# Two layers of memory attention and gMLP on one core: the lead units' turned features move into the tails of four block tiles, the second layer's first mixing operand lies over wo alone, and w_in's last load goes in two parts

## The chip, the cores and the metric

The kernel runs on one NeuronCore of one Trainium2 chip. The metric is the device time of one execution in microseconds. Every comparison is between executions of the kernel before and of another kernel on the same chip.

## The reference

Two layers run one after the other. Each is an attention with a running memory over 4 segments of 512 rows, followed by a gMLP. S = 2048 rows, D = 640, H = 32 heads of 20, Fh = 864.

```
# attention, per head and segment s: qs, ks, vs are 512 x 20; phi(t) = t + 1 for t > 0, else exp(t)
p     = softmax(qs ks^T * 20**-0.5 + mask)
num   = phi(qs) @ M                   # M, z: the memory of the segments before
o     = g * num / (phi(qs) @ z + 1e-6) + (1 - g) * p @ vs
M, z  = M + phi(ks)^T vs, z + sum(phi(ks))
x     = x + concat(o) @ wo            # q, k, v = layernorm(x) @ wq, wk, wv
# gMLP
z     = gelu(layernorm(x) @ w_in)     # 2048 x 1728
z1,z2 = z[:, :864], layernorm(z[:, 864:])
x     = x + (z1 * (w_sp @ z2 + b_sp)) @ w_out
```

## The kernel before

**Precision and tiles.** Values that go into TensorE are split into a high and a low float16 part, and a product is three matmuls (high·high, high·low, low·high). Rows come in 16 blocks t of 128. PSUM tiles are evicted by ACT and DVE; SP issues the loads, stores and transposes, all in one queue, in order.

**Phases of a layer.** `phase1a` is the attention (class `Attention`): a schedule in ticks, written by hand, lays the steps of each unit (scores, softmax, products with the values) on the engines. T is its last tick. Its late steps also carry work for what follows: the first row blocks of the gMLP's layernorm, and the load of the second half of w_in (`background`, weight `wi[0]`; the other half is `wi[1]`). The tiles of the last steps are PHL (the softmax, high and low), pv (its product with the values), oat (the divided output), ohl (its high and low part, stored to o), xt (rows of x with wo's product added, stored) and mr (row maxima for the next unit's operand qk).

`phase1b` takes each row block through the first half of the gMLP. `load` and `attn_out` bring or finish x1, layernorm gives xn. `xn_t` calls `split_t`: ACT casts the high part (L318), DVE subtracts for the low part (L319), one DMA transpose makes th (L320). `w_in_half` multiplies (zp, L395), first with `wi[1]`, then with `wi[0]` (its tile is named w in the profile). z2 is normalized and put by `blocks` into seven tiles zb, the sums and differences of a fast product scheme; z1 is stored (L409). `g.mark[i]` keeps the last instructions of step i, behind which early work of the next phase may stand on its engines (`behind`).

`phase2f` (layer 1) and `phase2s` (layer 2) mix the row blocks with w_sp: seven products per pair of blocks instead of eight (L800 and L548), then gating, and the product with w_out (cyp). w_sp's rows are scaled by their largest value, split (L764, L768, L527, L532) and turned by DMA transposes. Layer 1 stores half of the turned operand (turned), and layer 2 loads it (wt<-turned) instead of making it again. In `phase2f` a table of numbers sets the order of the items in each window: "L1" is the low half of the first combined operand (L794), "u1l" the item that ends with u<-d (L807), "P2" and "P3" the products into banks c and b.

The last window of `phase2f` also computes what layer 2's attention starts with: its two lead units' q and k (L1444), with the features phi(k) split into phl and turned into pk (L1487), and the values (L1388). mup (L1543) is the first that reads pk.

**Where the tiles lie.** SBUF has a left and a right stack of pools. On the right, from the edge, stand the tiles of `wi[1]` (17,280 bytes a partition) and of wo (12,800), then what a phase adds. Before the change layer 2's pk tiles were in a pool of 4 KB at the right edge (`nxt.pk`, pool "epk"), held until `phase2s`, and so everything that layer 2's `phase1b` puts on the right lay 4 KB further in than in layer 1, among it xnhl (pool "be1", one buffer). In `phase2s` the operand tiles wt lie on the right too: four in pt1 (16,384 bytes from the edge) and, behind it, the first two in pt0. Each zb tile has 6,912 columns; the lead units use 6,400 of them for other things, so that the last 512 are free there.

Of the kernel before, what the change touches and what calls it, by code (L numbers as in the profile page):

```python
# [9 lines left out]
F32 = mybir.dt.float32  # L10
F32R = mybir.dt.float32r
F16 = mybir.dt.float16
# [9 lines left out]
NT = S // 128  # L22
# [313 lines left out]
def phase1b(g, o_d, x, x1_d, z1_d, put, after):  # L336
    nc, tc = g.nc, g.tc
    first = not g.wu.made
    with ExitStack() as ctx:
# [66 lines left out]
        def z1_half(t, zp):  # L406
            z1 = p2.tile([128, FH], F32, tag="z1", name="z1")
            nc.scalar.activation(z1.rearrange("p (n c) -> p n c", n=2), zp[:, :, :FHH], AF.Gelu_apprx_tanh, scale=g.zi[0])
            return nc.sync.dma_start(z1_d[t], z1).ins  # L409
# [14 lines left out]
        for i, t in enumerate(ts):  # L424
            if i + 2 < NT:
                b = load(ts[i + 3]) if i + 3 < NT else None
                ths.append(xn_t(attn_out(ts[i + 2], *a)))
                a = b
            th = ths.pop(0)
            last = z2_half(t, w_in_half(1, *th))  # L430
            g.mark[i] = last
            sent = z1_half(t, w_in_half(0, *th))
            with tc.issue_after(last[1]), tc.issue_after(sent):
                if first and i in (7, 9):
                    g.wi[i == 7].keep()
                for _ in range(1 + (i < 4)):
                    next(more, None)
# [40 lines left out]
def phase2s(g, w_sp, x1_d, z1_d, zb, out):  # L478
# [6 lines left out]
    with ExitStack() as ctx:  # L485
        pool = lambda n, b, **k: ctx.enter_context(tc.tile_pool(name=n, bufs=b, reuse_waits="tile", **k))
        pr, ps, ph = pool("dr", 3), pool("ds", 2), pool("dh", 2)
        p2, px, pv, pu = pool("d2", 2), pool("dx", 3), pool("dv", 1), pool("du", 1)
        pt1, pt0 = pool("dtr1", 1, side="right"), pool("dtr0", 1, side="right")
        pg, py = pool("dg", 1, space=PSUM), pool("dy", 1, space=PSUM)  # L490
        small = lambda nm: g.small.tile([128, 1], F32, tag=nm, name=nm)
        un = g.small.tile([128, NT], F32, tag="unt", name="unt")
        nc.vector.tensor_scalar(un, g.wpw, 1.0 / (WB * ZB), None, ALU.mult)
        un = [un[:, t:t + 1] for t in range(NT)]
        raw, sums, split, ready = {}, {}, {}, {}

        def rows(t):
# [227 lines left out]
def phase2f(g, w_sp, x1_d, z1_d, zb, out, nxt, rest):  # L725
# [14 lines left out]
    psum = lambda n: pb_.enter_context(tc.tile_pool(name=n, bufs=1, space=PSUM, reuse_waits="tile"))  # L740
    pg, py = psum("fg"), psum("fy")
    small = lambda nm: g.small.tile([128, 1], F32, tag=nm, name=nm)
    un = g.small.tile([128, NT], F32, tag="unt", name="unt")
    raw, halves, wt, f = {}, {}, {}, {}

    def scale(t):
# [231 lines left out]
            item(n, k)  # L978
    wu = g.wu.bring()
    g.wu.made = True  # L980
    for w in range(NP):
        for n, lag in order:
            k = w - lag
            if not 0 <= k < NP or (n, k) in early:
                continue
            with tc.issue_after(g.parted) if w == 0 else ExitStack():
                item(n, k)
            if w == 0 and n in ("P2", "P3", "P5", "P6"):
                next(wu)
            if w + 1 == NP and n in ("P4", "P5", "P6"):  # L990
                a = "qkv"[int(n[1]) - 4]
                nc.sync.dma_start(g.wf[a], g.wkept[a])
                if n == "P5":
                    nxt.turned()
# [18 lines left out]

    run = lambda it: [None for _ in it]
    slots.close()
    nxt.pk = side(nxt.late, "epk", 2)
    halves_ = ExitStack()
    nxt.u2 = side(halves_, "eu2", 3)
    for nm, m, o in (("q", 0, "a"), ("k", 0, "b"), ("q", 1, "c"), ("k", 1, "d")):
# [105 lines left out]
class Attention:  # L1125
# [10 lines left out]
    def __init__(self, g, x, o_d, x1_d):  # L1136
        self.g, self.nc, self.tc = g, g.nc, g.tc
        self.x, self.o_d, self.x1_d = x, o_d, x1_d
        self.st = g.st
        self.xt, self.mst = g.xt, g.mst  # L1140
        self.ctx, self.late = ExitStack(), ExitStack()
        self.ln = {}
        self.gm, self.ot = {}, {}
        self.phq = {}
        self.P, self.Pf, self.mx = {}, {}, {}
        self.pv, self.o = {}, {}
        self.wait, self.last, self.stacked = [], -1, -1
        self.held, self.readout = {}, set()
        self.now, self.later, self.rd = None, {}, set()
        self.last_of, self.marks = {}, {}  # L1150
        self.half = None
        self.normed = {}
# [42 lines left out]
    def pool(self, n, b, **k):  # L1195
        return self.ctx.enter_context(self.tc.tile_pool(name=n, bufs=b, reuse_waits="tile", **k))

    def sbuf(self):
        g, pool = self.g, self.pool
        self.u2, sk, sv = pool("au2", 2), pool("ak", 1), pool("av", 1)  # L1200
        self.pk = self.u2
        self.vs = [values_tile(g, p) for p in (sv, sk)]
        self.qk = [sk.tile([128, 2, L], F16, name=f"qk{i}") for i in range(self.NQK - 1)] + [g.qk5]
        self.p3, self.pl2, self.bg, self.e2, self.pl1, self.u4 = pool("a3", 3), pool("al2", 2), pool("abg", 2), pool("ae2", 2), pool("al1", 1), pool("au4", 4)
        self.e1 = self.e2
# [250 lines left out]
    def out(self, nm, s, m, ps):  # L1456
# [25 lines left out]
        def keys():  # L1482
            hl = self.u2.tile([128, 2, L], F16, tag="hl", name="phl")
            nc.scalar.mul(hl[:, 0], ps, g.sig)
            nc.vector.scalar_tensor_tensor(hl[:, 1], ps, g.sig, hl[:, 0], ALU.mult, ALU.subtract)  # L1485
            pk = self.pk.tile([128, 2, 4, 128], F16, tag="pk", name="pk")
            nc.sync.dma_start(pk.rearrange("p i t c -> p (i t) c"), hl.rearrange("p i c -> p (i c)"), transpose=True)  # L1487
            if self.now is None:
                self.wait.append((s, m, pk))
            else:  # L1490
                self.post(3 if self.now > 0 else 5, lambda: self.update(s, m, pk), True)
# [39 lines left out]
    def update(self, s, m, pk):  # L1531
# [2 lines left out]
        for i in range(m, min(m + 2, NU)):  # L1534
            assert s < 2 or (s - 1, i) in self.readout, (s, m, i)
        self.held[(s + 1) % 2, m] = s + 1
        pkh, pkl = pk[:, 0], pk[:, 1]
        n = len(TH[m])
        hs = slice(TH[m][0], TH[m][0] + n)
        v = self.vs[s % 2]  # L1540
# [179 lines left out]
    def run(self, nseg=NSEG):  # L1720
# [81 lines left out]
        def background():  # L1802

            g, nc = self.g, self.nc
            wi = g.wi[0]
            wi.place(g.w0)
            if first:
                yield -8
                nc.sync.dma_start(g.bsp, self.b_sp.rearrange("(t p) -> p t", p=128))
                for i, a in enumerate("qkv"):  # L1810
                    yield 20 + 4 * i
                    nc.sync.dma_start(g.wkept[a], g.wf[a])
                yield 100
                yield from other_scales(g, self.ws, (wi,), 5, 101, 2.5, "ws")
                nc.vector.tensor_scalar(g.sc[:, 8:10], g.pw[:, 4:6], 2.0 ** -24, None, ALU.mult)
            yield T - 10.5
            pace = 0.5 if first else 0.9
            for i, _ in enumerate(wi.load(self.u2, FHH, ("hl", "tmp"), False, 1)):
                yield T - 10.3 + pace * i

        def weights():

# [95 lines left out]
def interleaved_layers(ctx, tc, x, wq, wk, wv, wo, beta, w_in, w_sp, b_sp, w_out, out):  # L1918
# [4 lines left out]
    g.bsp = cp.tile([128, NT], F32, tag="bsp", name="bsp")  # L1923
    g.wpw = cp.tile([128, NT], F32, tag="wpw", name="wpw")
    g.wiv = cp.tile([128, NT], F32, tag="wiv", name="wiv")
    attn_consts(g, cp, beta)
    attn_weights(g, ctx, cp, wv, wq, wk, wo, w_in, w_out)

# [15 lines left out]
    for i in range(2):  # L1944
        z1_d = [dram(f"z1_{i}_{t}", (128, FH)) for t in range(NT)]
        rest = ExitStack()
        with ExitStack() as top:
# [1 line left out]
            zp = rest.enter_context(tc.tile_pool(name="zr", bufs=1, reuse_waits="tile"))  # L1949
            zb = {**g.zb, **{j: zp.tile([128, 2, NT // 2, FHH], F16, name=f"zb{j}") for j in ZREST}}  # L1950
            phase1b(g, o_d[i], xs[i], x1_d[i], z1_d, blocks(g, zb), att[i].after)
        if i:
            att[1].late.close()
        if i:
            phase2s(g, w_sp, x1_d[i], z1_d, zb, xs[i + 1])
            rest.close()
# [28 lines left out]
```

## Time and profile before

| | |
|---|---|
| runs | 2213.96, 2214.73, 2215.64 us; median 2214.73 |
| the profiled execution | 2213.89 us, span 2212.2 us, granted TensorE clock 0.982 |
| TensorE busy | 2075.9 us, 94% of the span, 19725 matmuls |
| VectorE, ScalarE, GpSimd busy | 74%, 55%, 49% |
| DMA | 358.38 MB, mean 162 GB/s |

A row of a list of instructions has the start, the duration, the engine, the line, the operation, what it writes and reads, the count of those run together, and in brackets the idle time of the engine just before, with what ended it. Times count from the span's start. Layer 1's attention runs to about 596 us, its `phase1b` to about 790, its `phase2f` to about 1170; layer 2's attention to about 1654, its `phase1b` to about 1865, and `phase2s` to the end.

### The profile page before, as it was taken

The numbers are of one execution on the slowest core, as the hardware profiler recorded it, in microseconds if no ns is written. First come the engines' busy times: TensorE is split into PE (matmuls) and PEld (weight loads), VectorE is DVE, ScalarE is ACT, GpSimd is POOL, SyncE is SP. The second block draws the span as 40 slices with busy tenths as digits, with TensorE's granted clock in tenths as the row PEclk, the third lists the DMA queues.
The fourth block names the chain that finished last, engine by engine and source line by source line (L and its number), as shares of the span: only waits on it lengthen the run. The fifth ranks groups of instructions, "written<-read, shape, count | busy, mean of one in ns | idle before, by whom it ended". The sixth has DMA issues, their size and how long they took to land.

```text
span 2212.2 us, 48897 instructions
## 1 busy us (share of the span) xinstructions
PE 2075.9 (94%) x19725; PEld 1252.5 (57%) x19725; DVE 1626.2 (74%) x2952; ACT 1221.0 (55%) x1490; POOL 1084.3 (49%) x704
## 2 busy tenths in 40 slices
PE   4888899999899999999999999999987998999999
PEld 2455565666555545555665556566654554555555
DVE  8678888787778888999647887877764675465464
ACT  3499888788634433233225998888862344222221
POOL 2298988888424433433313987788861242000000
PEclk9999999999999999999999999999998999999999
DMA  5626635456767887888774353345565334988884
GB/s 165 186 65 207 154 91 143 109 133 151 197 169 186 236 212 195 234 243 212 204 210 112 89 136 86 110 112 143 136 187 133 90 103 122 261 204 204 228 208 114
DMA packets 516435, 358.38 MB, mean 162 GB/s; under 512 B 410096, under 2 KB 452656, under 8 KB 511088
## 3 DMA queue, kind: packets, MB, share of 16 engines
q1 hardware_dynamic: 516208, 355.26, 61.0%
q8 instruction: 154, 2.52, 0.5%
q14 instruction: 73, 0.60, 0.1%
HBM read 159.65 MB, written 107.43 MB: 121 GB/s over the span
## 4 chain that ended last, share of the span: by engine, by line
PE 69%; DVE 9%; ACT 9%; issue 5%; DMA 5%; POOL 3%; SPq 1%; POOLq 0%; ACTq 0%; DVEq 0%
PE zp L395 16%; PE cyp L596 4%; PE cyp L871 4%; ACT P L1624 3%; PE gb L548 3%; PE pv L1677 3%; PE yps L1420 3%; PE ga L548 3%; PE vps L1388 3%; PE qps L1444 3%; PE a L800 3%; PE b L800 3%; PE mp L1617 3%; ACT PHL L1642 2%; PE kps L1444 2%
## 5 line engine op out<-in xcount | busy, mean ns | idle before, releaser
L1643 POOL TENSOR_TENSOR PHL<-P,PHL 128x1024 f16<-128x1024 f32 x310 | 660.0, 2137 | 182.0 <-ACT PHL L1642 136.8
L1624 ACT ACTIVATE P<-es,sc 128x1024 f32<-128x1024 f32 x320 | 356.5, 1114 | 93.8 <-PE es L1588 91.8
L1634 DVE TENSOR_REDUCE mx<-mp 128x2 f32<-128x1024 f32 (+2 forms) x384 | 321.2, 862 | 84.4 <-PE mp L1588 83.4
L1642 ACT CAST PHL<-P 128x1024 f16<-128x1024 f32 x320 | 333.9, 1044 | 6.3
L395 PEld LDWEIGHTS <-th 128*128 128x128 f16 x1920 | 188.6, 98 | 180.2 <-DMA th<-xnhl 16.7
L1677 PEld LDWEIGHTS <-PHL 128*128 128x128 f16 x5120 | 166.7, 96 | 58.4 <-DVE oat L1698 18.7
L800 PEld LDWEIGHTS <-wt 128*128 128x128 f16 x1344 | 132.2, 98 | 118.7 <-DVE wt L794 4.4
L548 PEld LDWEIGHTS <-wt 128*128 128x128 f16 x1344 | 131.8, 98 | 119.3 <-DMA wt<-wn 6.0
L395 PE MATMUL zp<-wi,th 128*128 128x432 f16 x960 | 183.2, 350 | 16.6 <-DVE lnve L305 16.6
L306 POOL TENSOR_TENSOR lnrs<-lnve,mhalf 128x1 f32<-128x1 f32 x78 | 49.9, 648 | 299.7 <-DVE lnve L305 249.7
L1677 PE MATMUL pv<-vs,PHL 128*128 128x41 f16 x5120 | 172.5, 181 | 21.2 <-DVE oat L1698 17.4
L395 PE MATMUL zp<-w,th 128*128 128x432 f16 x960 | 180.4, 346 | 0.0
L1444 PEld LDWEIGHTS <-zb 128*128 128x128 f16 x1200 | 103.3, 99 | 102.7 <-issue 8.7
L785 POOL TENSOR_TENSOR f<-wt 128x1024 f32<-128x1024 f16 x32 | 79.7, 2494 | 139.5 <-DVE wt L794 111.4
L1617 PEld LDWEIGHTS <-qk 64*128 64x128 f16 (+1 forms) x1728 | 65.5, 93 | 127.1 <-issue 94.0
L1617 PE MATMUL mp<-qk 60*128 60x512 f16 (+3 forms) x864 | 108.2, 304 | 17.5 <-DVE mx L1634 11.9
L1420 PE MATMUL yps<-wo,o 128*128 128x320 f16 x720 | 122.0, 307 | 0.0
L1617 PE MATMUL es<-qk 64*128 64x256 f16 (+3 forms) x864 | 106.4, 298 | 9.1 <-ACT P L1624 6.5
L871 PE MATMUL cyp<-w,ut 128*128 128x320 f16 (+1 forms) x630 | 88.1, 299 | 0.0
L1388 PE MATMUL vps<-zb,w 128*128 128x320 f16 x480 | 82.8, 304 | 4.5 <-DVE phl L1485 4.5
L764 ACT ACTIVATE wn<-wr,wiv 128x1024 f16<-128x1024 f32 x32 | 36.6, 1145 | 90.4 <-DVE wiv L752 40.3
L1631 DVE TENSOR_REDUCE mx<-mp 128x4 f32<-128x1024 f32 x64 | 77.8, 1215 | 11.2 <-PE mp L1588 11.1
(313 smaller groups left out, 4220.0 us busy)
## 6 DMA issues: line engine op xcount, KB each, us to landing
wr<-in_B_w_sp_dram SPq DMA_DIRECT2D x32, 1024.0 KB
qk<-st SPq DMA_DIRECT2D x216, 120.0 KB
z<-z SPq DMA_DIRECT2D x32, 432.0 KB
cz<-z SPq DMA_DIRECT2D x32, 432.0 KB
turned<-wt SPq DMA_DIRECT2D x24, 512.0 KB
wt<-turned SPq DMA_DIRECT2D x24, 512.0 KB
st<-qhl SPq DMA_DIRECT2D x40, 256.0 KB
st<-khl SPq DMA_DIRECT2D x40, 256.0 KB
```

The lines of the kernel that those rows point to most:

```text
L395: nc.tensor.matmul(zp[:, n, :FHH], a[:, k, :], b[:, k, c:c + FHH], start=(k == 0 and j == 0), stop=(k == KD - 1 and j == 2))
L548: nc.tensor.matmul(o[:, :FHH], wt[:, x, m, :], zb[b][:, y, m, :], start=start and i == j == 0, stop=i == NP - 1 and j == 2, skip_group_che ...
L800: nc.tensor.matmul(o[:, :FHH], w[:, x, m, :], zb[b][:, y, m, :], start=start and i == j == 0, stop=i == NP - 1 and j == 2, skip_group_chec ...
L871: nc.tensor.matmul(yp[n][:, :320], a[:kn[k], k, :], b[:kn[k], k, n * 320:(n + 1) * 320], start=(k == 0 and j == 0), stop=(k == KO - 1 and ...
L1420: nc.tensor.matmul(ps, a[:, k, :], b[:, k, c], start=(i == 0), stop=(i == 14))
L1444: nc.tensor.matmul(ps, a[:, k, c], b[:, k, :], start=(i == 0), stop=(i == 14))
L1617: nc.tensor.matmul(out[:, h, o:o + w], a[r, ac], b[r, bc], start=o == 0, stop=False, skip_group_check=True)
L1624: self.last_of["ACT"] = nc.scalar.activation(self.Pf[t], es, AF.Exp, scale=g.esc).ins
L1634: self.last_of["DVE"] = nc.vector.tensor_reduce(mx[:, e, :, i], mp[:, :, o:o + w], AX.X, ALU.max).ins
L1642: nc.scalar.copy(hl[:, 0], P)
L1643: (nc.gpsimd if t < self.T - self.TAIL or t % 2 == 0 else nc.vector).tensor_tensor(hl[:, 1], P, hl[:, 0], ALU.subtract)
L1677: nc.tensor.matmul(pv[:, i, h, 0:PVC - 1], self.P[u][:, x, h, o:o + 128], v[:, j, h0 + h, :], start=first and h == x == 0 and (u, o, i, j) ...
```

## The change

1. The pool "epk" goes. Four of the zb tiles (0, 3, 4, 1) give their last 512 columns to the lead units' pk: one half (high or low) of one unit to each. A unit's features are turned by two DMA transposes of 128x4x128 instead of one of 128x8x128. Later units keep their own tile.
2. In `phase2s` a pad "dp" of 896 bytes stands ahead of pt1, so that pt1 ends where `wi[1]` ends, and pt0 lies over wo alone.
3. The load of `wi[0]` in `background` begins at T − 28 instead of T − 10.5: in layer 1 its first eight steps (a load or a split each), in layer 2 its first four, two ticks apart; the rest follows from T − 10.3.
4. `g.mark[i]` also holds z1's store and the last block difference on POOL, so that early items of `phase2f` and `phase2s` stand behind these on SP and POOL.
5. In the first window of `phase2f` the item ("L1", −1) stands right behind ("u1l", 0).
6. The scales `un` are a constant tile, filled in layer 1 and read in layer 2, which made them again before.

```diff
--- before.py
+++ after.py
@@ -428,8 +428,8 @@
                 a = b
             th = ths.pop(0)
             last = z2_half(t, w_in_half(1, *th))
-            g.mark[i] = last
             sent = z1_half(t, w_in_half(0, *th))
+            g.mark[i] = *last, sent, g.parted
             with tc.issue_after(last[1]), tc.issue_after(sent):
                 if first and i in (7, 9):
                     g.wi[i == 7].keep()
@@ -486,12 +486,11 @@
         pool = lambda n, b, **k: ctx.enter_context(tc.tile_pool(name=n, bufs=b, reuse_waits="tile", **k))
         pr, ps, ph = pool("dr", 3), pool("ds", 2), pool("dh", 2)
         p2, px, pv, pu = pool("d2", 2), pool("dx", 3), pool("dv", 1), pool("du", 1)
+        pool("dp", 1, side="right").tile([128, 224], F32, name="dp")
         pt1, pt0 = pool("dtr1", 1, side="right"), pool("dtr0", 1, side="right")
         pg, py = pool("dg", 1, space=PSUM), pool("dy", 1, space=PSUM)
         small = lambda nm: g.small.tile([128, 1], F32, tag=nm, name=nm)
-        un = g.small.tile([128, NT], F32, tag="unt", name="unt")
-        nc.vector.tensor_scalar(un, g.wpw, 1.0 / (WB * ZB), None, ALU.mult)
-        un = [un[:, t:t + 1] for t in range(NT)]
+        un = [g.un[:, t:t + 1] for t in range(NT)]
         raw, sums, split, ready = {}, {}, {}, {}
 
         def rows(t):
@@ -740,7 +739,7 @@
     psum = lambda n: pb_.enter_context(tc.tile_pool(name=n, bufs=1, space=PSUM, reuse_waits="tile"))
     pg, py = psum("fg"), psum("fy")
     small = lambda nm: g.small.tile([128, 1], F32, tag=nm, name=nm)
-    un = g.small.tile([128, NT], F32, tag="unt", name="unt")
+    un = g.un
     raw, halves, wt, f = {}, {}, {}, {}
 
     def scale(t):
@@ -978,8 +977,10 @@
             item(n, k)
     wu = g.wu.bring()
     g.wu.made = True
+    first = [x for x in order if x != ("L1", -1)]
+    first.insert(first.index(("u1l", 0)) + 1, ("L1", -1))
     for w in range(NP):
-        for n, lag in order:
+        for n, lag in order if w else first:
             k = w - lag
             if not 0 <= k < NP or (n, k) in early:
                 continue
@@ -1013,7 +1014,8 @@
 
     run = lambda it: [None for _ in it]
     slots.close()
-    nxt.pk = side(nxt.late, "epk", 2)
+    ends = [g.zb[j].rearrange("p i m c -> p (i m c)")[:, -512:].rearrange("p (t c) -> p t c", c=128) for j in ZA]
+    nxt.places = [ends[:2], ends[2:]]
     halves_ = ExitStack()
     nxt.u2 = side(halves_, "eu2", 3)
     for nm, m, o in (("q", 0, "a"), ("k", 0, "b"), ("q", 1, "c"), ("k", 1, "d")):
@@ -1138,7 +1140,7 @@
         self.x, self.o_d, self.x1_d = x, o_d, x1_d
         self.st = g.st
         self.xt, self.mst = g.xt, g.mst
-        self.ctx, self.late = ExitStack(), ExitStack()
+        self.ctx, self.places = ExitStack(), []
         self.ln = {}
         self.gm, self.ot = {}, {}
         self.phq = {}
@@ -1198,7 +1200,6 @@
     def sbuf(self):
         g, pool = self.g, self.pool
         self.u2, sk, sv = pool("au2", 2), pool("ak", 1), pool("av", 1)
-        self.pk = self.u2
         self.vs = [values_tile(g, p) for p in (sv, sk)]
         self.qk = [sk.tile([128, 2, L], F16, name=f"qk{i}") for i in range(self.NQK - 1)] + [g.qk5]
         self.p3, self.pl2, self.bg, self.e2, self.pl1, self.u4 = pool("a3", 3), pool("al2", 2), pool("abg", 2), pool("ae2", 2), pool("al1", 1), pool("au4", 4)
@@ -1483,8 +1484,14 @@
             hl = self.u2.tile([128, 2, L], F16, tag="hl", name="phl")
             nc.scalar.mul(hl[:, 0], ps, g.sig)
             nc.vector.scalar_tensor_tensor(hl[:, 1], ps, g.sig, hl[:, 0], ALU.mult, ALU.subtract)
-            pk = self.pk.tile([128, 2, 4, 128], F16, tag="pk", name="pk")
-            nc.sync.dma_start(pk.rearrange("p i t c -> p (i t) c"), hl.rearrange("p i c -> p (i c)"), transpose=True)
+            if self.places:
+                pk = self.places.pop(0)
+                for i in range(2):
+                    nc.sync.dma_start(pk[i], hl[:, i], transpose=True)
+            else:
+                pk = self.u2.tile([128, 2, 4, 128], F16, tag="pk", name="pk")
+                nc.sync.dma_start(pk.rearrange("p i t c -> p (i t) c"), hl.rearrange("p i c -> p (i c)"), transpose=True)
+                pk = pk[:, 0], pk[:, 1]
             if self.now is None:
                 self.wait.append((s, m, pk))
             else:
@@ -1534,7 +1541,7 @@
         for i in range(m, min(m + 2, NU)):
             assert s < 2 or (s - 1, i) in self.readout, (s, m, i)
         self.held[(s + 1) % 2, m] = s + 1
-        pkh, pkl = pk[:, 0], pk[:, 1]
+        pkh, pkl = pk
         n = len(TH[m])
         hs = slice(TH[m][0], TH[m][0] + n)
         v = self.vs[s % 2]
@@ -1813,10 +1820,10 @@
                 yield 100
                 yield from other_scales(g, self.ws, (wi,), 5, 101, 2.5, "ws")
                 nc.vector.tensor_scalar(g.sc[:, 8:10], g.pw[:, 4:6], 2.0 ** -24, None, ALU.mult)
-            yield T - 10.5
-            pace = 0.5 if first else 0.9
-            for i, _ in enumerate(wi.load(self.u2, FHH, ("hl", "tmp"), False, 1)):
-                yield T - 10.3 + pace * i
+            n, pace = (9, 0.85) if first else (5, 0.9)
+            yield T - 28
+            for i, _ in enumerate(wi.load(self.u2, FHH, ("hl", "tmp"), False, 1), 1):
+                yield T - 28 + 2 * i if i < n else T - 10.3 + pace * (i - n)
 
         def weights():
 
@@ -1923,6 +1930,7 @@
     g.bsp = cp.tile([128, NT], F32, tag="bsp", name="bsp")
     g.wpw = cp.tile([128, NT], F32, tag="wpw", name="wpw")
     g.wiv = cp.tile([128, NT], F32, tag="wiv", name="wiv")
+    g.un = cp.tile([128, NT], F32, tag="un", name="un")
     attn_consts(g, cp, beta)
     attn_weights(g, ctx, cp, wv, wq, wk, wo, w_in, w_out)
 
@@ -1950,8 +1958,6 @@
             zb = {**g.zb, **{j: zp.tile([128, 2, NT // 2, FHH], F16, name=f"zb{j}") for j in ZREST}}
             phase1b(g, o_d[i], xs[i], x1_d[i], z1_d, blocks(g, zb), att[i].after)
         if i:
-            att[1].late.close()
-        if i:
             phase2s(g, w_sp, x1_d[i], z1_d, zb, xs[i + 1])
             rest.close()
         else:
```

The order of the instructions follows. TensorE's rows stand as before. ACT at the end of layer 2's attention, before: the last softmax casts, the last output cast, and then the three casts of row blocks for th, the load of the gelu's table and the first gelu.

```order
L1642 CAST PHL<-P 128x1024
L1624 ACTIVATE P<-es,sc 128x1024
L1642 CAST PHL<-P 128x1024
L1708 CAST ohl<-oat 128x640
L318 CAST xnhl<-x_25822 128x640
L318 CAST xnhl<-x_25834 128x640
L318 CAST xnhl<-x_25841 128x640
L401 ACT_TABLE_LOAD
L401 ACTIVATE z_25906<-zp_25875,sc 128x864
```

The same engine after, in two pieces: behind the last mr, some eight PHL casts earlier, and at the end.

```order
L1659 ACTIVATE mr<-mtp 16x128
L318 CAST xnhl<-x_25819 128x640
L1649 CAST PHL<-P 128x1024
L1631 ACTIVATE P<-es,sc 128x1024
```

```order
L1631 ACTIVATE P<-es,sc 128x1024
L318 CAST xnhl<-x_25831 128x640
L1649 CAST PHL<-P 128x1024
L318 CAST xnhl<-x_25838 128x640
L1715 CAST ohl<-oat 128x640
L401 ACT_TABLE_LOAD
```

The first cast has moved ahead of eight of the softmax casts, the second ahead of the last of them, the third ahead of the last output cast.

SP at the end of layer 2's `phase1b`, before: z1's stores, then the loads of turned operands, then the transposes of the new ones (wn is their split form).

```order
L409 DMA z_1_9<-z_27467 128x864
L409 DMA z_1_10<-z_27550 128x864
L539 DMA wt<-turned_1 128x2048
L539 DMA wt<-turned_0 128x2048
L539 DMA wt<-turned_1 128x2048
L500 DMA wr<-in_B_w_sp_dram 128x2048
L409 DMA z_1_11<-z_27643 128x864
L541 DMA_TRANSPOSE wt<-wn 128x16x128 x3
```

SP after, in the middle of `phase1b` and at its end:

```order
L409 DMA z_1_15<-z_26836 128x864
L499 DMA wr<-in_B_w_sp_dram 128x2048 x2
L538 DMA wt<-turned_0 128x2048
L320 DMA_TRANSPOSE th<-xnhl 128x10x128
L354 DMA x_26939<-x_1_8 128x640
L409 DMA z_1_4<-z_26936 128x864
L540 DMA_TRANSPOSE wt<-wn 128x16x128
L320 DMA_TRANSPOSE th<-xnhl 128x10x128
```

```order
L409 DMA z_1_10<-z_27547 128x864
L538 DMA wt<-turned_1 128x2048
L540 DMA_TRANSPOSE wt<-wn 128x16x128
L538 DMA wt<-turned_1 128x2048
L499 DMA wr<-in_B_w_sp_dram 128x2048
L409 DMA z_1_11<-z_27640 128x864
L540 DMA_TRANSPOSE wt<-wn 128x16x128
```

One load of a turned operand and one transpose have moved among the th transposes, and the next transpose stands behind the first of the late loads.

DVE in the first window of layer 1's `phase2f`, before: L1's instruction is the last row (f is the combined row block, wt its high and low half).

```order
L844 TENSOR_TENSOR u<-u,cz_12798 128x864
L768 SCALAR_TENSOR_TENSOR wn<-wr,wiv,wn 128x1024
L848 TENSOR_REDUCE uam<-u 128x1
L807 SCALAR_TENSOR_TENSOR u<-e,unt,u 128x432
L852 TENSOR_SCALAR upw<-uam 128x1
L853 TENSOR_SCALAR upw<-upw 128x1
L854 RECIPROCAL uiv<-upw 128x1
L855 TENSOR_SCALAR uiv<-uiv 128x1
L856 TENSOR_SCALAR xs<-upw,pw 128x1
L794 TENSOR_TENSOR wt<-f_12753,wt 128x1024
```

After, the two last rows of the item u1l and what follows:

```order
L806 SCALAR_TENSOR_TENSOR u<-d,un,q_12825 128x432
L793 TENSOR_TENSOR wt<-f_12753,wt 128x1024
L748 TENSOR_SCALAR wpw<-am 128x1
L749 TENSOR_SCALAR wpw<-wpw 128x1
L750 RECIPROCAL wiv<-wpw 128x1
L751 TENSOR_SCALAR wiv<-wiv 128x1
L752 TENSOR_SCALAR un<-wpw 128x1
L843 TENSOR_TENSOR u<-u,cz_12798 128x864
L767 SCALAR_TENSOR_TENSOR wn<-wr,wiv,wn 128x1024
L847 TENSOR_REDUCE uam<-u 128x1
L806 SCALAR_TENSOR_TENSOR u<-e,un,u 128x432
```

It has moved from behind the gating's scales (uiv, xs) to right behind u<-d, ahead of fourteen others.

## The prediction

> **What bounds the kernel now.** First the time shares: TensorE is busy for 94% of the span, so the kernel is its matmuls plus the places where it stands still. I therefore read TensorE's busy time stage by stage (busy time and instruction count of PE, PEld, DVE, ACT, POOL, then the granted clock, DMA share, GB/s), and then its waits inside each stage. Two stages of several: most of layer 1's attention, and the passage from attention to the gMLP's first half in layer 2, where TensorE works 51 of 72 us at a granted clock of 0.84.
>
> ```profile
> 60.00:540.00 480.00, 439.05 (x5992) 278.87 (x5992) 379.85 (x783) 391.03 (x486) 390.51 (x233) 0.98 0.52 137
> 1600.00:1672.00 72.00, 51.14 (x715) 35.00 (x713) 42.17 (x90) 40.44 (x42) 38.41 (x23) 0.84 0.72 194
> ```
>
> The waits of TensorE (total us, times, longest) in 540 to 600, then in 790 to 840, in 1600 to 1672, and in 1858 to 1885:
>
> ```profile
> PE pv L1677 <- DVE oat L1698: 7.3, 2, 5.4
> PE mtp L1650 <- DVE mx L1631: 2.2, 1, 2.2
> ...
> PE c L800 <- DVE wt L794: 4.0, 1, 4.0
> ...
> PE zp L395 <- DVE lnve L305: 16.6, 1, 16.6
> PE pv L1677 <- DVE oat L1698: 2.3, 1, 2.3
> PE mtp L1650 <- DVE lnve L305: 1.9, 1, 1.9
> ...
> PE gc L548 <- DMA wt<-wn: 5.5, 1, 5.5
> ```
>
> The change touches all four places. The largest, 16.6 us, is in layer 2 only: layer 1's first zp starts with no wait at all.
>
> **E: layer 2's first w_in product (the 4 KB that go).** TensorE at both passages, layer 1 first; columns are start, duration, engine, line, operation, count, idle before.
>
> ```profile
> 596.51 5.64 PE L395 MATMUL zp<-wi,th 128*128 128x432 f16 x30
> 601.99 5.64 PE L395 MATMUL zp<-w,th 128*128 128x432 f16 x30
> ...
> 1653.50 0.57 PE L1677 MATMUL pv<-vs,PHL 128*128 128x41 f16 x16
> 1670.69 8.41 PE L395 MATMUL zp<-wi,th 128*128 128x432 f16 x30 [16.62 <-DVE lnve L305]
> 1678.94 5.64 PE L395 MATMUL zp<-w,th 128*128 128x432 f16 x30
> ```
>
> After the gap the first thirty matmuls take 1678.94 − 1670.69 = 8.25 us from start to start, against 601.99 − 596.51 = 5.48 in layer 1: 2.8 us go to the lower clock. What zp needs is th, the turned high and low half of the first normalized row block. Its making in layer 1 (first row) and in layer 2:
>
> ```profile
> 567.63 0.73 ACT L318 CAST xnhl<-x 128x640 f16<-128x640 f32 x1 [0.94 <-DVE x L312]
> ...
> 1631.57 2.41 DVE L312 TENSOR_SCALAR x<-x,lnmv,lnrs 128x640 f32<-128x640 f32 x1 [0.37 <-POOL lnrs L306]
> 1662.90 0.73 ACT L318 CAST xnhl<-x 128x640 f16<-128x640 f32 x1 [5.25 <-DMA o<-ohl]
> 1663.66 0.82 DVE L319 TENSOR_TENSOR xnhl<-x,xnhl 128x640 f16<-128x640 f32 x1 [8.38 <-ACT xnhl L318]
> 1666.19 1.38 SPq L320 DMA_TRANSPOSE th<-xnhl  x1
> ```
>
> In layer 1 the cast runs 29 us before zp. In layer 2 the first row blocks are normalized by 1634.0, and the cast waits until 1662.9 for attention's last output stores (o<-ohl): xnhl lies over their source, because the lead units' 4 KB at the right edge push layer 2's tiles down. That zp's wait is booked on lnve is chance: lnve ends as th lands, 4.5 us after its issue. Without the 4 KB the tiles lie as in layer 1, and the changed order puts the cast among the attention's PHL casts, behind mr. Then th lands by about 1634.0 + 0.7 + 0.8 + 4.5 = 1640, 13 us before the last pv. Gain: 16.6 + 2.8 = 19.4. Against it, the casts and the L319 subtractions (0.7 and 0.8 us, two each) and the second norm now lie inside the last attention steps. Layer 1, which lives like that, has 7.3 + 2.2 = 9.5 us of waits there, layer 2 has 2.3 + 1.9 = 4.2; the cost is between 1.5 (the extra DVE work alone, twice 0.8) and 5.3 (layer 1's waits). I take 3, nearer the middle since part of layer 1's waits is its w_in splitting, which layer 2 does not do. E = 16.4, between 12 (14.1 less a second, shorter wait) and 18.
>
> On the clock, the Trainium skill (TensorE: Matmul & The Clock Gate, Part 1) says that the array falls to half its clock after an idle window of about 3.4 us and comes back after about 3.4 us of work; an estimate from that page is a loss of 1.7 us after each such gap. The trace shows 2.8 lost here and 1.3 at gc below, so it agrees in kind and not in size. By the page E and F together would be 0.7 us smaller.
>
> **F: layer 2's first mixing products (dp).** TensorE, then the queue:
>
> ```profile
> 1857.67 1.99 PE L395 MATMUL zp<-wi,th 128*128 128x432 f16 x10
> ...
> 1875.05 5.86 PE L548 MATMUL gc<-zb,wt 128*128 128x432 f16 x24 [5.54 <-DMA wt<-wn]
> 1880.74 4.54 PE L548 MATMUL gb<-zb,wt 128*128 128x432 f16 x24
> ...
> 1870.59 8.51 SPq L541 DMA_TRANSPOSE wt<-wn  x3
> ```
>
> gc waits for operand block 1, whose transpose is issued at 1870.59 and lands 4.46 later. With the 896-byte dp the first two operand tiles lie over wo alone, which is read last by t = 15; the changed order has block 0's load and block 1's transpose some 50 us earlier, among the th transposes. So the 5.54 go, and with them 5.86 − 4.54 = 1.3 of clock (gc against gb): 6.8. What is late next is block 2 (gb): it still lies over w_in's half, but its transpose now goes out first, behind the last zp on that half (wi, done by 1859.7), and at 4.5 to 8.5 us from about 1862 it lands by 1870.5; gb would start at 1875.05 − 5.54 + 4.4 = 1873.9. The one inserted transpose is 1.4 to 2.8 us of queue ahead of the next th (8.51 for three); th is made two row blocks ahead, over 20 us of zp. F = 6.8, between 4 (block 2 late by its whole margin) and 6.9.
>
> **A: layer 1's last attention steps (w_in in two parts).** DVE ahead of the two late oat, the price of a split on ACT and on DVE, and the queue:
>
> ```profile
> 570.02 2.27 DVE L312 TENSOR_SCALAR x<-x,lnmv,lnrs 128x640 f32<-128x640 f32 x1
> 573.41 0.31 DVE L1698 TENSOR_TENSOR oat<-pv,rs 128x160 f32<-128x160 f32 x1
> 578.68 0.89 DVE L303 BATCH_NORM_STATS2 lnst<-x 128x6 f32<-128x320 f32 x2 [2.24 <-DMA x<-x]
> 579.48 2.18 DVE L91 SCALAR_TENSOR_TENSOR w<-wst,iv,w 128x432 f16<-128x432 f32 x1
> 582.77 0.32 DVE L1698 TENSOR_TENSOR oat<-pv,rs 128x160 f32<-128x160 f32 x1
> ...
> 559.25 0.65 ACT L90 ACTIVATE w<-wst,iv 128x432 f16<-128x432 f32 x1
> ...
> 568.78 0.66 DVE L91 SCALAR_TENSOR_TENSOR w<-wst,iv,w 128x432 f16<-128x432 f32 x1
> ...
> 557.06 1.41 SPq L172 DMA_DIRECT2D wst<-in_B_w_in_dram  x3
> ```
>
> The first oat comes behind a norm (2.27) and an L319, the second behind statistics that wait 2.24 for a load and a split of 2.18. In the changed order both oat stand ahead of these, and four or five of the ten splits run before 540. That would take 2.3 + 0.8 from the first wait and up to 2 from the second: 5 at most. But moved splits cost 0.65 us on ACT and 0.66 on DVE each, in a stretch where ACT is 81% and DVE 79% busy and TensorE loses 41 us: 5 × 0.65 = 3.3 if all of it shows. A = 2, between −3 and 5. In layer 2 the early part is five plain loads at about 0.47 us of queue each (1.41 for three), and nothing splits there: nothing lost while no fetch stands behind a held one.
>
> **C: the first window of layer 1's mixing (L1 of pair 1 earlier).**
>
> ```profile
> 827.56 6.97 PE L800 MATMUL c<-zb,wt 128*128 128x432 f16 x22 [3.96 <-DVE wt L794]
> 834.37 4.54 PE L800 MATMUL b<-zb,wt 128*128 128x432 f16 x24
> 838.75 3.42 PE L871 MATMUL cyp<-w,ut 128*128 128x320 f16 x24
> ...
> 820.56 0.66 DVE L807 SCALAR_TENSOR_TENSOR u<-d,unt,q 128x432 f32<-128x432 f32 x1
> 826.29 1.22 DVE L794 TENSOR_TENSOR wt<-f,wt 128x1024 f16<-128x1024 f32 x1
> 830.20 1.22 DVE L794 TENSOR_TENSOR wt<-f,wt 128x1024 f16<-128x1024 f32 x1
> ...
> 821.15 1.03 ACT L791 CAST wt<-f 128x1024 f16<-128x1024 f32 x1
> ```
>
> c waits for the L794 at 826.29. Moved behind u<-d it can run when its cast is done, 822.2 to 823.4, so c runs on at 823.5 and ends near 827.5: 3.96 of wait and 2.8 of clock (6.81 for 22 against 4.38 for 24) seem won. But the fourteen DVE instructions that stood ahead now come 1.1 to 2 us later, among them uiv, for which ACT waits before it makes the next high part; so the L794 now at 830.20 ends near 832.5, and b, which needs it, waits 5 us and restarts at the low clock: 832.5 + 4.4 + 2.8 = 839.7, where it ended at 838.75 before. C = −1, between −1.5 and 6.8 (b not waiting).
>
> **Nothing on the path.**
>
> ```profile
> 1145.99 1.25 SPq L1487 DMA_TRANSPOSE pk<-phl  x1
> ...
> 1165.21 0.23 PE L1543 MATMUL mup<-vs,pk 128*128 128x147 f16 x1
> ```
>
> The lead units' features: four half transposes for two on the queue, 1.25 us more per unit; the second unit's is read 19 us after its issue, and the matmuls between cover it; bare, the two would cost 2.5 us. The un row computed once saves one DVE operation of 16 columns beside full TensorE. The marks let phase 2's early items start later behind z1's store and the last difference; TensorE has no wait between 600 and 790, which covers it; uncovered, bounded by one such transpose, 2.8 us.
>
> **Sum.** 2213.89 (this execution: span 2212.2 and 1.7 around it) − 16.4 − 6.8 − 2 + 1 = 2189.7. The median of the runs, 2214.73, is 0.84 above it: about 2190.
>
> **Rivals.**
> (1) E is cut short: th is made on time, but another transfer of the queue (the last o<-ohl pair, w_in's second half) holds it or the second th, and only a third of 19.4 comes, 6.5: 2200. For it: the cast's row shows that this passage waits on transfers; against: layer 1 with the same places has no such wait.
> (2) Layer 2's last steps become as bound to DVE as layer 1's, and A brings nothing: E = 14, 2213.89 − 14 − 6.8 + 1 + 0.84 = 2195.
> (3) b does not wait because the cast it needs is ordered ahead: C = 6.8, 2182.
> (4) Block 2 becomes what block 1 was: F = 0, 2197.
> (5) Slower. The early loads of w_in stand in one queue with the fetches of the next unit (qk<-mr, qk<-st). If a held stage tile keeps that queue, the unit is late and TensorE with it. It turns slower when the ten early pieces of both layers cost 2.4 us of TensorE each (24.2 over ten); their own issue and split are 0.47 + 2 × 0.65 = 1.8, and all of them would have to show, so it needs further waits. ACT at 81% speaks for some of it, not for that much.
> (6) The cast still waits as before and block 1 too, from another overlap: 2214.
>
> **How the numbers follow.** Forecast 0.46; (1) 0.12; (2) 0.15; (3) 0.13; (4) 0.07; (5) 0.04; (6) 0.03. The range 2179 to 2203 holds the forecast with its terms' bounds and rivals 1 to 4, and leaves out 5, 6 and pairs of mishaps. 0.2%, 4.4 us, is about what a measurement of this kernel can tell from no change. Faster 0.92, same 0.04, slower 0.04: only (5) ends above 2219, and (6) with the mildest of (5) lies within.
>
> **What the next profile would show.** E: the wait of zp in layer 2 is gone, the xnhl cast stands 15 us or more before the last pv, th issued before it; wrong if zp still waits over 3 us. F: no wait of gc, wt<-wn well before 1850; a wait of gb instead is rival 4. A: the two waits of pv in layer 1 sum to less than 5; more waits between 460 and 540 is the price. C: c without a wait, and b with one of about 5 us. The prediction fails if TensorE's waits between 60 and 540, or between 1180 and 1600, grow by more than 5 us.

## The result and the profile after

The changed kernel takes 2196.41 us (median of 4, 2195.07 to 2197.64) against 2214.35 before: a ratio of 0.9922, 95% interval 0.9905 to 0.9939. The forecast was 2190, so 18 us came of the 24 that were expected. The profiled executions, 2213.89 and 2197.64 us with spans of 2212.2 and 2195.9, differ by 16.3, and what follows accounts for those.

TensorE's waits in the profile after, in 540 to 600, in 600 to 790, in 790 to 840 and in 1600 to 1672 (line numbers of the same code differ by up to seven from before's); after 1672 no wait of over 0.1 us is listed:

```profile
PE pv L1684 <- DVE oat L1705: 3.5, 1, 3.5
PE mtp L1657 <- DVE mx L1638: 1.8, 1, 1.8
...
PE zp L395 <- ACT z L408: 5.0, 3, 2.6
...
PE c L799 <- ACT wt L790: 3.0, 1, 3.0
PE b L799 <- ACT wt L790: 2.2, 1, 2.2
PE b L799 <- DVE wt L793: 0.7, 1, 0.7
PE c L799 <- DVE wpw L748: 0.7, 1, 0.7
...
PE pv L1684 <- DVE oat L1705: 5.6, 2, 2.8
PE mtp L1657 <- DVE mx L1638: 1.7, 1, 1.7
PE es L1624 <- ACT P L1631: 1.5, 2, 1.3
```

The 16.6 of zp in layer 2 and the 5.5 of gc are gone. New is a wait of zp in layer 1, where there was none, and the window behind it waits 6.6 instead of 4.0. The same is read from the starts of TensorE's stages, in the order of the program:

```profile
593.10 5.64 PE L395 MATMUL zp<-wi,th 128*128 128x432 f16 x30
...
790.05 1.26 PE L799 MATMUL a<-zb,wt 128*128 128x432 f16 x6
...
844.78 5.46 PE L870 MATMUL cyp<-w,ut 128*128 128x320 f16 x39
...
1664.20 5.63 PE L395 MATMUL zp<-wi,th 128*128 128x432 f16 x30 [0.24 <-DVE xt L1427]
1669.67 5.64 PE L395 MATMUL zp<-w,th 128*128 128x432 f16 x30
...
1855.70 4.54 PE L547 MATMUL ga<-zb,wt 128*128 128x432 f16 x24
1864.46 4.54 PE L547 MATMUL gb<-zb,wt 128*128 128x432 f16 x24
```

| stretch | before, us | after, us | difference | forecast |
|---|---|---|---|---|
| start to layer 1's first zp (A) | 596.51 | 593.10 | −3.4 | −2 |
| to the first mixing product a (marks) | 191.52 | 196.95 | +5.4 | 0 |
| to the first cyp (C) | 50.72 | 54.73 | +4.0 | +1 |
| to layer 2's first zp (E, the wait) | 831.94 | 819.42 | −12.5 | −13.6 |
| the first thirty of zp (E, the clock) | 8.25 | 5.47 | −2.8 | −2.8 |
| to ga | 186.03 | 186.03 | 0 | 0 |
| ga to gb (F) | 15.77 | 8.76 | −7.0 | −6.8 |
| to the end of the span | 331.46 | 331.44 | 0 | 0 |

E and F came in the sizes that were worked out (F from another cause, as the experiments show), with the signs that were named: the cast of xnhl runs at 1636.55, th goes out at 1642.89, 21 us ahead of zp, and gc's transpose goes out at 1786.36. TensorE's waits in the two attentions hardly grew: from 40.0 to 42.2 us between 60 and 540, from 21.1 to 21.4 between 1180 and 1600.

```profile
1636.55 0.73 ACT L318 CAST xnhl<-x 128x640 f16<-128x640 f32 x1 [1.60 <-DVE x L312]
...
1642.89 1.59 SPq L320 DMA_TRANSPOSE th<-xnhl  x1
...
1786.36 1.32 SPq L540 DMA_TRANSPOSE wt<-wn  x1
```

What was missed lies in layer 1's `phase1b`, in the stretch that the prediction called covered. ACT (two pieces) and then TensorE there, in the profile after:

```profile
757.03 0.83 ACT L90 ACTIVATE whl<-wst,iv 128x640 f16<-128x640 f32 x1 [5.07 <-DMA wst<-in_B_w_out_dram]
...
758.91 0.97 ACT L408 ACTIVATE z<-zp,sc 128x864 f32<-128x864 f32 x1
...
769.57 0.83 ACT L90 ACTIVATE whl<-wst,iv 128x640 f16<-128x640 f32 x1 [3.96 <-DMA wst<-in_B_w_out_dram]
...
772.60 0.97 ACT L408 ACTIVATE z<-zp,sc 128x864 f32<-128x864 f32 x1
...
759.93 5.64 PE L395 MATMUL zp<-w,th 128*128 128x432 f16 x30 [1.46 <-ACT z L408]
...
773.62 5.63 PE L395 MATMUL zp<-w,th 128*128 128x432 f16 x30 [2.58 <-ACT z L408]
```

ACT splits the pieces of w_out here (L90, into whl). Six of its seven splits wait for their load, 17.8 us in all, where before three waited 7.8 us; and L408, which empties zp for the tile w, stands behind such splits. This half of w_in has only one PSUM tile for zp, so TensorE stops. The pieces run late: the queue issues the first of these loads at 707.80, against 665.34 before (that line was L885):

```profile
665.34 0.38 SPq L885 DMA_DIRECT2D wst<-in_B_w_out_dram  x1
```

```profile
707.80 0.74 SPq L884 DMA_DIRECT2D wst<-in_B_w_out_dram  x1
```

Six parts of the change could cause that, so the experiments take them apart. Each kernel ran four to eleven times. A difference between two kernels below is one of ratios to before times 2214.6 us; each ratio's interval is about ±0.0015, 3 us, unless it is given.

### The profile page after: what moved, and what is told of

It is laid out like the page before. It is cut to its first block, busy times and chain, and to the rows that moved or that the text cites. A ratio compares the mean times of both kernels' runs of the same rounds, so it can differ in the third digit from the quotient of the medians.

```text
span 2195.9 us, 48888 instructions
## 1 busy us (share of the span) xinstructions
PE 2067.9 (94%) x19725; PEld 1250.9 (57%) x19725; DVE 1625.9 (74%) x2951; ACT 1217.8 (55%) x1490; POOL 1086.5 (49%) x704
## 4 chain that ended last, share of the span: by engine, by line
PE 66%; DVE 11%; ACT 8%; DMA 5%; issue 5%; POOL 4%; SPq 1%; ACTq 0%; DVEq 0%; POOLq 0%
PE zp L395 13%; PE cyp L595 4%; PE cyp L870 4%; PE ga L547 3%; PE gb L547 3%; PE yps L1421 3%; PE pv L1684 3%; PE b L799 3%; PE a L799 3%; PE qps L1445 3%; ACT P L1631 3%; PE vps L1389 3%; PE mp L1624 3%; PE kps L1445 2%; POOL PHL L1650 2%
## 5 line engine op out<-in xcount | busy, mean ns | idle before, releaser
L784 POOL TENSOR_TENSOR f<-wt 128x1024 f32<-128x1024 f16 x32 | 84.8, 2660 | 127.5 <-DVE wt L793 110.0
L1595 PE MATMUL es<-big,maskk 64*128 64x128 f16 (+1 forms) x1280 | 82.4, 206 | 1.5 <-issue 1.5
```

## Experiments: the marks

The changed kernel with the old marks, and the kernel before with the new ones:

```diff
-            g.mark[i] = *last, sent, g.parted        # e1_marks_old
+            g.mark[i] = last
```

```diff
-            g.mark[i] = last                          # e6_marks_alone, on the kernel before
+            g.mark[i] = *last, sent, g.parted
```

> The changed kernel with g.mark[i] = last as before (part 4 undone). Theory: the longer marks push w_out's split pieces and the first turned operands to later steps of layer 1's phase1b, where ACT's L90 waits for its load ahead of L408 and so holds zp (5.0 us in three waits); the same lateness moves the first window of phase2f by about 4 us more. With the old marks the three waits of zp are gone, c runs without a wait and b waits about 5: 2188, between 2186 and 2190. Rival: the bunching comes from elsewhere (L1's place, the un tile), the waits stay: 2196. Second rival: layer 2 needs the marks, its early load of a turned operand holds th: over 2196.

> The kernel before with the longer marks alone (part 4). Theory: they cost what undoing them brought, 5 us of zp's waits on ACT's L408 in layer 1 and up to 4 in the window behind: 2219 to 2223. Rival: they cost only beside the other parts: 2214.

Measured: 2188.28 us with the marks undone, ratio 0.9882 (0.9868 to 0.9895), 8.9 less than the changed kernel; and 2220.07 with the marks alone, 1.0029 (1.0019 to 1.0039), 6.4 us slower than before with an interval of 4.2 to 8.6. The first profile lists no wait of TensorE between 600 and 780. The second has the three of the changed kernel, on nothing but the marks:

```profile
750.02 5.63 PE L395 MATMUL zp<-w,th 128*128 128x432 f16 x30 [1.25 <-ACT z L408]
762.47 5.63 PE L395 MATMUL zp<-w,th 128*128 128x432 f16 x30 [1.34 <-ACT z L408]
776.23 5.63 PE L395 MATMUL zp<-w,th 128*128 128x432 f16 x30 [2.65 <-ACT z L408]
```

So part 4 is what cost, alone and with the rest. Which of its two additions does it?

```diff
-            g.mark[i] = *last, sent, g.parted
+            g.mark[i] = *last, sent                   # e7_mark_z1_only
+            g.mark[i] = *last, g.parted               # e8_mark_parted_only
```

> The changed kernel with marks that hold the last norm and z1's store, without the block difference. Theory: z1's store is what holds w_out's first piece on SP, so ACT's rows stay bunched, zp waits 5 us on L408 as in the changed kernel: 2196. Rival: the block difference on POOL is what delays: 2188, no waits of zp.

> The changed kernel with marks that hold the last norm and the block difference, without z1's store. Theory: SP and ACT stand as with the old marks, zp in layer 1 waits nowhere: 2188. Rival: POOL's later start alone delays the operands (L784) and the window behind: 2192 to 2196.

Measured: 2196.73 (0.9922, as the changed kernel) and 2188.88 (0.9887, as with the old marks); the waits of zp in 600 to 780 sum to 3.7 and to 0.2. The first load of w_out, with z1's store alone in the mark and with the difference alone:

```profile
709.82 0.73 SPq L884 DMA_DIRECT2D wst<-in_B_w_out_dram  x1
```

```profile
666.21 0.38 SPq L884 DMA_DIRECT2D wst<-in_B_w_out_dram  x1
```

It is z1's store. Early items of `phase2f` on SP, w_out's first load among them, wait for their turn behind it, all later pieces follow from the first, and their splits on ACT fall into steps where L408 needs the engine. ACT waits 17.2 us for these loads in the one and 3.2 in the other. From layer 1's first zp to a, the five kernels with z1's store in the mark take 197.0 to 199.1 us, the other nine 191.5 to 191.9: the store costs 5 to 7.6 us in this stretch, each time.

## Experiments: the 4 KB and the pad

> The changed kernel without the pad dp. Theory: the first two operand tiles lie over w_in's half again, gc waits 5 to 6 us for the transpose and runs at the low clock: 2196.4 + 6.8 = 2203. Rival: without the 4 KB of the lead units the tiles come free early anyway: 2196.

The changed kernel without the pad, which the prediction held to be F's cause:

```diff
-        pool("dp", 1, side="right").tile([128, 224], F32, name="dp")
```

Measured: 2197.45 us, 0.993 (0.9916 to 0.9943), 1.8 more than with it, which is within the intervals, and the rival's 2196 is the nearer one. gc does not wait; ga does, for 0.41:

```profile
1852.44 4.55 PE L546 MATMUL ga<-zb,wt 128*128 128x432 f16 x24 [0.41 <-DMA wt<-turned]
1856.83 4.54 PE L546 MATMUL gc<-zb,wt 128*128 128x432 f16 x24
1861.21 4.54 PE L546 MATMUL gb<-zb,wt 128*128 128x432 f16 x24
```

With that, part 1 was put alone on the kernel before (the diff of the tails, `nxt.places` and `late`, as in the change):

> The kernel before with part 1 alone: the lead units' features lie in the tails, the 4 KB are gone, nothing else is changed. Theory, after the kernel without dp showed no wait of gc: the 4 KB held both gains, E (14.2 of wait and 2.8 of clock, 17) and F (7), because with them the second operand tile lay over w_in's half and without them over wo: 2214.4 - 24 = 2190, zp's and gc's waits of layer 2 gone. Rival: E alone comes from part 1 and F from another part (marks or w_in's load): 2197 with gc waiting about 5. Second rival: w_in's early part is needed for E: 2200 or more.

Measured: 2189.93 us, 0.9892 (0.9877 to 0.9906). Part 1 alone gives more than the whole change, and both stalls are gone. From cyp to layer 2's first zp it takes 815.20 us where the kernel before takes 831.94, and from ga to gb 8.77 where that takes 15.77.

```profile
1655.93 5.64 PE L395 MATMUL zp<-wi,th 128*128 128x432 f16 x30
...
1847.78 4.55 PE L548 MATMUL ga<-zb,wt 128*128 128x432 f16 x24 [0.19 <-DMA wt<-turned]
1852.17 4.54 PE L548 MATMUL gc<-zb,wt 128*128 128x432 f16 x24
```

What held gc when the kernel ran was not its tile. Before, w_in's half was read for the last time by 1859.7, but gc's transpose went out only at 1870.59. The queue waited 4.9 us for the split of that operand, which ACT and DVE had made behind the last row block's casts (the first three rows, of the kernel before). With part 1 alone the first of the two splits runs at 1771.86, and the transposes go out right behind the first loads (the last two rows):

```profile
SPq L541 <- DVE wn L532: 4.9, 1, 4.9
1868.26 1.99 ACT L527 CAST wn<-s 128x1024 f16<-128x1024 f32 x2
1869.34 2.36 DVE L532 TENSOR_TENSOR wn<-s,wn 128x1024 f16<-128x1024 f32 x2
```

```profile
1771.86 1.04 ACT L527 CAST wn<-s 128x1024 f16<-128x1024 f32 x1
...
1842.99 6.55 SPq L541 DMA_TRANSPOSE wt<-wn  x2
```

All three kernels with the 4 KB make these casts 3.3 us behind the start of ga; all eleven without make the first one 72 to 76 us ahead of it. So the 4 KB decide where the splits stand on ACT; through which tile they do so is not shown.

The pad does what part 2 says, but it was not needed. Of the first two operand tiles, gc's is the one nearer the edge, from 16,384 to 20,480 bytes. Without the 4 KB and without the pad `wi[1]` still reaches to 17,280, so gc's transpose goes out only behind the last read of that half, from 1842.99 on here. That is in time. With the pad it goes out at 1786.36, and only ga gains by that, 0.2 to 0.4 us.

## Experiments: L1's place

> The kernel before with L1 of pair 1 in its new place alone (part 5). Theory, the prediction's C: c runs without a wait, b waits 4 to 5 us and restarts slowly, sum 0: 2214 to 2216. Rival: b is ready in time and the wait of c with its slow clock is saved: 2207 to 2209.

The kernel before with this alone:

```diff
+    first = [x for x in order if x != ("L1", -1)]
+    first.insert(first.index(("u1l", 0)) + 1, ("L1", -1))
...
-        for n, lag in order:
+        for n, lag in order if w else first:
```

Measured: 2215.6 us, ratio 1.0005 (0.9997 to 1.0014). c runs on, and b stands still and slow in its place:

```profile
825.02 4.54 PE L800 MATMUL c<-zb,wt 128*128 128x432 f16 x24
833.39 0.54 PE L800 MATMUL b<-zb,wt 128*128 128x432 f16 x2 [3.82 <-ACT wt L791]
834.67 5.81 PE L800 MATMUL b<-zb,wt 128*128 128x432 f16 x22 [0.74 <-DVE wt L794]
```

From a to cyp this profile has 50.3 us, before's 50.7. Then the old place in the changed kernel, with the new marks and with the old ones:

```diff
-    first = [x for x in order if x != ("L1", -1)]
-    first.insert(first.index(("u1l", 0)) + 1, ("L1", -1))
+    first = order
```

> The changed kernel with L1 of pair 1 in its old place in the first window (part 5 undone). Theory: the 6.6 us of waits of c and b come mainly from the late transposes, so c alone waits, about as long in sum: 2195 to 2198, zp's 5.0 us in layer 1 unchanged. Rival: L1's new place is what costs, and the window falls back to a wait of 4.0: 2193 or less.

> The changed kernel with parts 4 and 5 undone. Theory: the window of phase2f is as in the kernel before (c waits 4.0, then b without a wait), the waits of zp in layer 1 are gone: 2187, within 1.5 of the kernel with only the marks undone, since L1's new place trades a wait of c for one of b (the prediction's C = 1 us of loss). Rival: L1's new place brings up to 6.8 once its operands are early: then this one is 5 to 8 us slower than with only the marks undone.

Measured: 2194.82 (0.9917) and 2185.23 us (0.9871, 0.9857 to 0.9886). The second is 2.4 less than with the marks alone undone, within the intervals: L1's place is worth nothing to 3 us of loss. The first is 1.1 less than the changed kernel, within the intervals, and keeps zp's waits (5.4). From a to cyp the kernels with the old marks take 50.03 us (new place) and 49.95 (old place).

The 4.0 that the changed kernel's profile lost in this window are thus not the move's. Two rows, ACT in the profile after and before:

```profile
808.53 1.15 ACT L763 ACTIVATE wn<-wr,wiv 128x1024 f16<-128x1024 f32 x1 [5.15 <-DMA wt<-wn]
```

```profile
802.30 1.15 ACT L764 ACTIVATE wn<-wr,wiv 128x1024 f16<-128x1024 f32 x1 [2.95 <-DMA wt<-wn]
```

The row stands 18.5 us behind the first a, where before it stood 14.3 behind. The transposes come later, and everything behind them. With z1's store in the mark this window took 54.7, 50.2 (old place of L1), 50.7 (no pad), 53.0 (z1's store alone) and 55.4 us (marks alone); none of the others took over 51.2. The two kernels whose window lost nothing are those that lost most before it, 199.1 and 198.9 us from zp to a. From zp to cyp the five take 249.3 to 252.7 us, the other nine 239.1 to 242.7. So what z1's store costs falls partly into the window and partly before it, about 9 us together by the means, near the 6.4 to 8.9 of the medians.

## Experiments: w_in in two parts

> Parts 1, 2 and 6 on the kernel before: old marks, L1 in its old place, w_in's last load in one part from T - 10.5 (part 3 undone as well). Theory: part 3 is worth the difference of layer 1's passage, where the waits of pv and mtp in 540 to 600 go from 9.7 back up and the first zp of layer 1 starts 1.5 to 3.4 us later: 2187.5 to 2189 against 2185.2 for the kernel with the two-part load. Rival: the part-1-alone kernel's 2190 came from the missing pad, and the load's parts give nothing: 2185.

> Parts 1, 3 and 6 on the kernel before: old marks, old place of L1, no pad. Theory: the pad saves ga's wait for the first turned operand, 0.4 us, and no more: 2185.6. Rival: 2188 or more, if the later load of the first two operands pushes others back.

Both start from the last kernel (parts 1, 2, 3, 6):

```diff
-            n, pace = (9, 0.85) if first else (5, 0.9)      # e9_one_load
-            yield T - 28
...
+            yield T - 10.5
+            pace = 0.5 if first else 0.9
```

```diff
-        pool("dp", 1, side="right").tile([128, 224], F32, name="dp")     # e10_load_no_dp
```

Measured: 2190.14 us (0.9894, 0.9879 to 0.9908) with the load in one part, 2185.86 (0.987, 0.985 to 0.9889) with two parts and no pad. Part 1 alone, also with one part, had 0.9892; so two kernels with one part stand at 0.9892 and 0.9894, two with two at 0.9870 and 0.9871. By these four the two-part load is worth about 5 us, somewhat more than the first theory gave it, but each single pair of intervals overlaps, and the two without z1's store in the mark and with L1's new place, which have two parts too, stand at 0.9882 and 0.9887. By the start of layer 1's first zp it is worth 3.7: on average 594.5 us in the eight kernels with two parts, 598.2 in the five with one, where single executions lie up to 7 us apart. Parts 2 and 6 together bring nothing that can be measured (0.9894 with them, 0.9892 without). In 540 to 605 the waits with one part and with two:

```profile
PE pv L1683 <- DVE oat L1704: 6.3, 4, 3.8
PE mtp L1656 <- DVE mx L1637: 2.2, 1, 2.2
PE pv L1683 <- DVE PHL L1649: 1.1, 1, 1.1
```

```profile
PE mtp L1656 <- DVE mx L1637: 2.5, 1, 2.5
PE pv L1683 <- DVE oat L1704: 2.3, 2, 2.1
PE pv L1683 <- DVE PHL L1649: 0.4, 1, 0.4
```

9.6 against 5.2. More of it in the early part, twelve steps 1.4 ticks apart for eight steps 2 apart:

```diff
-            n, pace = (9, 0.85) if first else (5, 0.9)
+            n, pace = (13, 0.85) if first else (5, 0.9)
...
-                yield T - 28 + 2 * i if i < n else T - 10.3 + pace * (i - n)
+                yield T - 28 + 1.4 * i if i < n else T - 10.3 + pace * (i - n)
```

> Parts 1, 2, 3 and 6, old marks, old place of L1; w_in's first part in layer 1 has twelve steps 1.4 ticks apart instead of eight 2 apart. Theory: two more loads and splits leave the last steps, whose waits (about 5 us in 540 to 600) fall by at most 2, while the same work shows in part in the attention: 2184 to 2186, not to be told from 2185.2. Rival: the earlier splits hold ACT and DVE in the attention, 2188.

Measured: 2190.91 us, 0.9895 (0.988 to 0.991), 5 more. That is the rival's side, but the profiled executions are only 1.0 apart in span (2187.8 and 2186.8), and the waits in 540 to 605 sum to 7.0 against 5.2; whether the denser part costs 1 or 5 us is not settled. It too has two parts, and its 0.9895 is as slow as one part's, so the worth of the two parts is known only roughly.

## Why the prediction was right, and where not

The time lies in the range and on the forecast side, 6.4 us above the forecast. By its steps:

- E: right in mechanism and size. 15.3 in this profile; its wait and its clock are those named, and the waits of the last attention steps rose from 4.2 to 9.0 (forecast 3 more, bound 5.3). The reason for that rise is not the one given, or not it alone: with part 1 and w_in's load in one part these waits sum to 5.7 and 4.8, and E is 19.5 with part 1 alone, while the nine kernels with two parts have 5.1 to 9.0. The moved casts cost about 1 us; what brings the rest in some kernels is open, and w_in's early loads in layer 2, priced at nothing, are a candidate.
- F: right in size (7.0 for 6.8), wrong in cause. The step "with the 896-byte dp the first two operand tiles lie over wo alone" is true, and block 1's transpose went out earlier for it, but gc had waited for the split of its operand and not for the tile, and part 1 removed that wait. The pad's own price is 0.4 us or less. The prediction's rows showed it: the half was free by 1859.7, and the transpose went out 11 us later. That the number held is luck, since both parts came in one change.
- A: 3.4 in this profile and some 4 to 5 by the kernels without the two parts, for 2; towards the upper bound. The waits of 540 to 600 fell by 3.3 of the 5 that were thought possible, and those of 460 to 540, the price that was named, rose from 2.9 to 4.4 against 3.3. That rise may be no price at all: two kernels with one part have 3.7 and 4.8 there.
- C: right as a mechanism of its own: c waits no more and b waits 4.6 us, sum +1 us with an interval that holds 0. In the full change c waited again (3.7) and the window lost 4.0, which goes with z1's store in the mark.
- The marks: the step that failed. "TensorE has no wait between 600 and 790, which covers it; uncovered, bounded by one such transpose, 2.8 us." The row of a stage without waits shows that nothing is late in the order that stands, not how much may be moved in it. I priced the items on SP that were marked and left out the items that follow from them: w_out's loads, their splits on ACT, and L408 behind those on the same engine. It cost 5.4 in this profile and 3 more in the window behind, and 6.4 to 8.9 by the medians, which is the whole miss.
- Of the rivals, (2) named the rise of layer 2's last waits, which came in part (4.8 of 5.3), but A, which it put at nothing, came in full; its 2195 lies nearest to the measured time, by luck. (1) and (3) to (6) did not occur. None named the marks.

On the restart clock: after zp's and gc's waits were gone, so were the 2.8 and 1.3 us, and b, where it waits in the kernel with L1's place alone, shows the price again: 840.32 − 834.67 = 5.65 us from its first slow row to cyp for 22 matmuls that take 4.01, 1.6 lost. The price is not fixed for a gap: zp in layer 2 loses 2.8 us behind its 16.62 before, 1.5 behind 16.60 with L1's place alone and 1.3 behind 14.20 with the marks alone, and gc behind 5.5 loses 1.3, 2.4 and 2.3. So the two clock terms are those of one execution, but their sum hardly changes: 4.1, 3.8 and 3.6. The estimate of 1.7 us from the Trainium skill (TensorE: Matmul & The Clock Gate, Part 1) lies within the values seen, 1.3 to 2.8 us.

The best kernels are those with parts 1, 3 and 6, with the pad (2185.23 us) or without it (2185.86): 1.3% below the kernel before and 0.5% below the changed one.

## What to carry to other kernels

Where tiles of one phase lie over those of the next, a few kilobytes at the edge decide which waits exist and can move instructions on an engine by some 75 us. Before a wait is put down to a tile's place, look what the late transfer itself waited for, and work out the neighbours for every intermediate version before a gain is put down to one edit. A stage in which the bounding engine never waits is no cover for moved work: follow what is moved to the last instruction that waits for it, and see what else stands behind that in the same engine's order. When a bundle gains, undo its parts one by one; here one of six gave more than all together by the medians, and one cost a quarter to a third of the gain.

## What was not expected of the hardware

Single profiled executions of nearly the same program differ by more than their parts are worth: the first zp of layer 1 starts at 593.10, 595.05, 597.39 and 592.87 us in kernels (the changed one; without marks and L1's place; with the block difference's mark; without marks, L1's place and pad) whose differences lie behind that point but for the place of a few loads. A part worth under 5 us could be told only by medians, and then barely.
